# A state-space scan beside a local attention on one core: frames of four tokens with scaled B and C, and masks on GpSimd

## The chip, the cores and the metric

The kernel runs on one core of one Trainium2 chip. The metric is the device time in microseconds (us) of one execution. The kernel before takes 249.55 us as the median of four runs. Each run is marked fast or slow: a run is slow when it lies more than 1.5% above the fastest of its kernel.

Names of the engines in the profile: PE does the matrix products (PEld is its weight load), DVE is the vector engine, ACT the scalar engine, POOL is GpSimd, and SP is the engine from which most transfers are issued.

## The reference, cut to what matters

The two halves of the output are independent. The inputs and the output are bf16; S is 2048 and the width is 448.

```python
# Part A: a diagonal complex state-space layer, 448 complex states
dt = exp(log_dt); Lam_bar = exp(dt * Lam)
B_bar = ((Lam_bar - 1) / Lam)[:, None] * Bmat
Bu = x @ B_bar.T                                   # complex
for t in range(2048):
    h = Lam_bar * h + Bu[t]                        # the scan
y = 2 * (hseq @ Cmat.T).real + x * Dskip

# Part B: attention, 16 heads of 28; token t sees t, t-2, ..., t-14
q, k, v = split(x @ wqkv)
logits = q . k at 8 positions with stride 2, times 28 ** -0.5; positions < 0 masked
o = softmax(logits) @ v;   out = o @ wo

output = concatenate([A, B], axis=-1)
```

In both kernels the complex state is kept as 128 partitions (64 real, 64 imaginary) times 7 groups m.

Of the kernel before, what the change touches and what calls it, by code (L numbers as in the profile page):

```python
# [11 lines left out]
AX = mybir.AxisListType  # L12
# [3 lines left out]
S = 2048  # L16
D = 448
T = 16
NCH = 128
KT = 4  # L20
KP = 112
H = 16
DH = 28
W = 8
DIL = 2
HALO = (W - 1) * DIL
JH = T * H
TJ = HALO + T
NM = 7
PL = 64  # L30
NST = 7
PAD = 64
MA = 4
# [3 lines left out]
COSC = [(-1.0) ** k / math.factorial(2 * k) for k in range(7, 0, -1)]  # L37


def _make_identity(nc, ident):  # L40
    n = ident.shape[0]
    nc.gpsimd.memset(ident, 0.0)
    nc.gpsimd.affine_select(
        out=ident, in_=ident, compare_op=ALU.not_equal, fill=1.0, base=0,
        pattern=[[-1, n]], channel_multiplier=1,
    )


class PartB:

    QB = 114
    HL = 14
    XP = 16
    XC = XP + S + 16
    NB = 18
    GROUPS = ((0, 4), (4, 4), (8, 4), (12, 4), (16, 2))

    def __init__(self, tc, B_x, B_wqkv, B_wo, out_b, ident, pool, psum):
        self.tc, self.nc = tc, tc.nc
        self.B_x, self.B_wqkv, self.B_wo, self.out_b = B_x, B_wqkv, B_wo, out_b  # L60
        self.ident, self.pool, self.psum = ident, pool, psum

    def loads(self):
        nc, pool = self.nc, self.pool
        self.xT = pool.tile([NCH, KT, self.XC], bf16, name="xbT_sb", tag="xbT")
        for c in range(2):
            rows = slice(1024 * c, 1024 * (c + 1))
            cols = slice(self.XP + 1024 * c, self.XP + 1024 * (c + 1))
            nc.sync.dma_start_transpose(self.xT[:, 0:3, cols], self.B_x[0, rows, 0:384])  # L69
            nc.sync.dma_start_transpose(self.xT[:, 3, cols], self.B_x[0, rows, 320:448])  # L70
        self.wn = pool.tile([NCH, KT, 3 * D], bf16, name="wqkv_nat", tag="wn")
        nc.gpsimd.memset(self.wn[0:64, 3, :], 0.0)
        nc.scalar.dma_start(self.wn[:, 0:3, :], self.B_wqkv[0:384].rearrange("(k p) c -> p k c", p=NCH))
        nc.scalar.dma_start(self.wn[64:128, 3, :], self.B_wqkv[384:448])

    def loads2(self):
        nc, pool = self.nc, self.pool
        self.wo_p = pool.tile([NCH, 4, D], bf16, name="wo_p")
        nc.gpsimd.memset(self.wo_p[:], 0.0)
        wo_v = self.B_wo.rearrange("(g h d) c -> h d g c", g=4, d=DH)  # L80
        for h in range(4):
            nc.scalar.dma_start(self.wo_p[32 * h:32 * h + DH, :, :], wo_v[h])

    def prep(self):
        nc, pool, V, G = self.nc, self.pool, self.nc.vector, self.nc.gpsimd
        G.memset(self.xT[:, :, 0:self.XP], 0.0)
        G.memset(self.xT[:, :, self.XP + S:], 0.0)
        self.wp = pool.tile([NCH, 2, KT, H, 32], bf16, name="wqk_p", tag="xin")
        G.memset(self.wp[:, :, :, :, DH:], 0.0)
        for w in range(2):  # L90
            V.tensor_copy(self.wp[:, w, :, :, 0:DH],
                          self.wn[:, :, w * D:(w + 1) * D].rearrange("p k (h d) -> p k h d", d=DH))
        self.qT = pool.tile([NCH, 4, S], bf16, name="qT")
        self.kT = pool.tile([NCH, 4, self.XC], bf16, name="kT")
        G.memset(self.kT[:, :, 0:self.XP], 0.0)
        G.memset(self.kT[:, :, self.XP + S:], 0.0)
        self.va = pool.tile([NCH, self.NB, H, 32], bf16, name="v_aug")
        G.memset(self.va[:, :, :, DH:], 0.0)
        self.ones = pool.tile([NCH, 2, 32], bf16, name="ones")
        G.memset(self.ones[:], 1.0)  # L100
        G.memset(self.ones[0:self.HL, 1, :], 0.0)
        self.mask = pool.tile([NCH, self.QB], bf16, name="mask")
        G.memset(self.mask[:], 0.0)
        for w in range(W):
            G.affine_select(out=self.mask[:], in_=self.mask[:], compare_op=ALU.not_equal, fill=1.0,
                            base=self.HL - DIL * w, pattern=[[1, self.QB]], channel_multiplier=-1)
        self.oT = pool.tile([NCH, 4, self.XC], bf16, name="oT", tag="xbT")

    def qk_proj(self, c):
        nc = self.nc  # L110
        n = 0
        for w in range(2):
            for hg in range(4):
                ps = self.psum.tile([NCH, 512], f32, name="qk_ps", tag="mm")
                for k in range(KT):
                    nc.tensor.matmul(ps[:], lhsT=self.wp[:, w, k, 4 * hg:4 * hg + 4].rearrange("p h d -> p (h d)"),  # L116
                                     rhs=self.xT[:, k, self.XP + 512 * c:self.XP + 512 * (c + 1)],
                                     start=(k == 0), stop=(k == KT - 1))
                if w == 0:
                    dst = self.qT[:, hg, 512 * c:512 * (c + 1)]  # L120
                else:
                    dst = self.kT[:, hg, self.XP + 512 * c:self.XP + 512 * (c + 1)]
                if n % 2 == 0:
                    nc.scalar.copy(dst, ps[:])  # L124
                else:
                    nc.vector.tensor_copy(dst, ps[:])  # L126
                n += 1

    def v_proj(self, g):
        nc = self.nc  # L130
        b0, nb = self.GROUPS[g]
        for b in range(b0, b0 + nb):
            c0 = self.QB * b + self.XP - self.HL
            ps = self.psum.tile([NCH, H, DH], f32, name="v_ps", tag="mm")
            for k in range(KT):
                nc.tensor.matmul(ps[:].rearrange("p h d -> p (h d)"), lhsT=self.xT[:, k, c0:c0 + NCH],  # L136
                                 rhs=self.wn[:, k, 2 * D:3 * D], start=(k == 0), stop=(k == KT - 1))
            if b % 2 == 0:
                nc.scalar.copy(self.va[:, b, :, 0:DH], ps[:])
            else:  # L140
                nc.vector.tensor_copy(self.va[:, b, :, 0:DH], ps[:])

    def unit(self, g, hg):
        nc, pool, V = self.nc, self.pool, self.nc.vector
        b0, nb = self.GROUPS[g]
        QB, XP, HL = self.QB, self.XP, self.HL
        scale = DH ** -0.5
        nq = [min(QB, S - QB * b) for b in range(b0, b0 + nb)]
        tot = sum(nq)
        sp = [self.psum.tile([NCH, 2, 512], f32, name="s_ps", tag="s") for _ in range(2)]  # L150
        for i in range(nb):
            b = b0 + i
            kc = QB * b + XP - HL
            for h in range(4):
                nc.tensor.matmul(sp[h // 2][:, h % 2, QB * i:QB * i + nq[i]],  # L155
                                 lhsT=self.kT[32 * h:32 * h + DH, hg, kc:kc + NCH],
                                 rhs=self.qT[32 * h:32 * h + DH, hg, QB * b:QB * b + nq[i]],
                                 start=True, stop=True, skip_group_check=True)
        pts = []
        for u in range(2):  # L160
            pt = pool.tile([NCH, 2, 4 * QB], bf16, name="pt", tag="pt", bufs=4)
            nc.scalar.activation(pt[:, :, 0:tot], sp[u][:, :, 0:tot], ACT.Exp, scale=scale)  # L162
            if tot == nb * QB:
                pv = pt[:, :, 0:tot].rearrange("p h (b q) -> p h b q", q=QB)
                V.tensor_tensor(pv, pv, self.mask[:].unsqueeze(1).unsqueeze(1).to_broadcast([NCH, 2, nb, QB]),  # L165
                                op=ALU.mult)
            else:
                pv = pt[:, :, 0:QB]
                V.tensor_tensor(pv, pv, self.mask[:].unsqueeze(1).to_broadcast([NCH, 2, QB]), op=ALU.mult)
                pv = pt[:, :, QB:tot]  # L170
                V.tensor_tensor(pv, pv, self.mask[:, 0:nq[1]].unsqueeze(1).to_broadcast([NCH, 2, nq[1]]), op=ALU.mult)
            pts.append(pt)
        po = self.psum.tile([NCH, 4 * QB], f32, name="o_ps", tag="mm")
        pd = self.psum.tile([NCH, 4 * QB], f32, name="d_ps", tag="mm")
        for i in range(nb):
            for h in range(4):
                nc.tensor.matmul(po[32 * h:32 * h + 32, QB * i:QB * i + nq[i]],  # L177
                                 lhsT=self.va[:, b0 + i, 4 * hg + h, :],
                                 rhs=pts[h // 2][:, h % 2, QB * i:QB * i + nq[i]],
                                 start=True, stop=True, skip_group_check=True)  # L180
        spl = ((0, QB, 1), (QB, tot, 0)) if b0 == 0 else ((0, tot, 0),)
        for lo, hi, o in spl:
            for h in range(4):
                nc.tensor.matmul(pd[32 * h:32 * h + 32, lo:hi], lhsT=self.ones[:, o, :],  # L184
# [30 lines left out]
    def attention(self):  # L215
        done = 0
        for g, (b0, nb) in enumerate(self.GROUPS):
            for hg in range(4):
                self.unit(g, hg)
# [385 lines left out]
```

## The kernel before: the parts that the change touches

Part A walks through 16 steps j. All 128 chunks of 16 tokens advance one step at a time; the state is carried by products with a high and a low part of a rotation matrix; each state goes to memory and is read back, corrected with the result of the scan over the chunks, and used for y.

```python
def _level1_step(self, j, prev, has_prev):              # 16 times
    for m in range(NM):
        for k in range(KT):                             # 28 products of 128 columns
            nc.tensor.matmul(reg(m), lhsT=self.Bcat[:, k, m, :], rhs=self.xT[:, k, j, :], ...)
    if has_prev:
        for m in range(NM):                             # 14 carry products
            nc.tensor.matmul(reg(m), lhsT=Lm[:, m, :], rhs=prev(m), ...)
            nc.tensor.matmul(reg(m), lhsT=Lm[:, NM + m, :], rhs=prev(m), ...)
    nc.scalar.copy(ht[:, 0:MA, :], psA[:])
    nc.scalar.copy(ht[:, MA:NM, :], psB[:])
...
# main(): states to memory and back, correction, y
for j in range(T):
    eng.dma_start(hin[:].rearrange("p m c -> p (m c)"), hs[j])
    for m in range(NM):
        nc.tensor.matmul(reg(m), lhsT=ident[:], rhs=hin[:, m, :], ...)
        nc.tensor.matmul(reg(m), lhsT=cm, rhs=g, ...)
    nc.scalar.copy(ht[:, 0:MA, :], psA[:]); nc.scalar.copy(ht[:, MA:NM, :], psB[:])
    ... # y from 7 products with Ccat and 4 with the skip, ACT copies it out
```

Part B works in 20 units: a group of up to four blocks of queries times one of four groups of heads. The mask is a DVE multiply, the denominators are products with ones, and the reciprocal is Ln and Exp on ACT.

```python
nc.scalar.activation(pt[...], sp[u][...], ACT.Exp, scale=scale)
V.tensor_tensor(pv, pv, self.mask[...].to_broadcast(...), op=ALU.mult)
...                                                     # o_ps: weights times v
for h in range(4):
    nc.tensor.matmul(pd[32 * h:32 * h + 32, lo:hi], lhsT=self.ones[:, o, :], rhs=pts[h // 2][...], ...)
nc.scalar.activation(r[:, 0:tot], pd[:, 0:tot], ACT.Ln)
nc.scalar.activation(r[:, 0:tot], r[:, 0:tot], ACT.Exp, scale=-1.0)
V.tensor_tensor(self.oT[...], po[:, 0:tot], r[:, 0:tot], op=ALU.mult)
```

The order in which the parts are written is: projections of B, weights of A, all of A, all of B's attention.

The softmax here doesn't subtract the row's maximum and nothing guards it: scores larger than these inputs give would overflow.

## Time and profile before

| | before |
|---|---|
| median time | 249.55 us (248.87 to 250.39, 4 runs) |
| span of the profiled run | 247.0 us |
| PE, DVE, ACT, POOL busy | 199.7, 67.9, 139.0, 36.3 us |
| written to memory | 7.34 MB |

From the page of the kernel before: busy time of each engine (with its share of the span and its instructions), and the chain of waits that ended last, by engine.

```profile
PE 199.7 (81%) x2261; PEld 127.5 (52%) x2261; DVE 67.9 (27%) x157; ACT 139.0 (56%) x261; POOL 36.3 (15%) x54
...
PE 47%; ACT 24%; issue 11%; DVE 8%; SPq 7%; DMA 2%; ACTq 0%
```

The windows view of the kernel before gives, for each stretch from:to, its length, the busy us of each engine (x is the count of instructions), the granted clock of PE as a share of full speed, the DMA share and GB/s.

```profile
0.00:37.00 37.00, 16.48 (x64) 6.05 (x65) 16.44 (x66) 7.84 (x15) 13.59 (x41) 0.92 0.85 166
37.00:71.00 34.00, 33.65 (x156) 15.51 (x156) 18.04 (x25) 13.83 (x21) 22.75 (x13) 0.93 0.10 36
71.00:85.00 14.00, 12.39 (x168) 10.19 (x166) 0.62 (x1) 13.79 (x29) 0.00 (x0) 1.00 0.12 49
85.00:120.00 35.00, 35.00 (x630) 35.00 (x627) 1.27 (x2) 17.05 (x35) 0.00 (x0) 1.00 0.34 113
120.00:136.00 16.00, 11.37 (x181) 9.74 (x177) 0.00 (x0) 11.58 (x25) 0.00 (x0) 1.00 0.09 31
136.00:181.00 45.00, 38.75 (x386) 25.95 (x386) 0.00 (x0) 21.86 (x47) 0.00 (x0) 1.00 0.37 106
181.00:247.00 66.00, 52.04 (x692) 25.07 (x688) 31.51 (x64) 53.04 (x93) 0.00 (x0) 0.79 0.09 31
```

The order of the five busy columns is PE, PEld, DVE, ACT, POOL. PE is busy 33.65 of 34 us in B's projections and 35.00 of 35 in level 1 of A; ACT is busy 13.79 of 14 in the set-up between them; in the attention at the end PE and ACT share the load. DVE and POOL stand idle for whole stages.

These are lines of the timeline of before on DVE and on POOL around 38 us (start, duration, engine, line, operation):

```profile
37.89 3.23 DVE L165 TENSOR_TENSOR pt<-pt,mask 128x912 bf16<-128x912 bf16 x1
...
37.45 3.19 POOL L384 TENSOR_TENSOR Lmat<-Dm,Shl 128x1792 bf16<-128x1792 f32 x1 [1.14 <-DVE gs L398]
```

The mask multiply takes 0.744 us on the mean of its 32 executions, but 3.23 us when it meets a POOL instruction of 3.19 us: it ended only after the POOL instruction had.

### The profile page before, as it was taken

The page shows a single profiled execution, that of the slowest core. Times are in us where ns is not written, and L with a number is a line of the kernel's source. Part 1 is how long each engine was busy: PE and PEld are TensorE (multiplying, and loading weights), DVE is VectorE, ACT ScalarE, POOL GpSimd, SP SyncE. Part 2 cuts the span into 40 slices and gives each one's busy share as a digit, 9 for nine tenths or more (in the row PEclk, how much of TensorE's full clock was granted, in tenths as well). Part 3 has the DMA queues.
Part 4 walks back from the last instruction along what each step waited for, and adds up shares of the span by engine and source line. Part 5 has one row for each costly group of instructions (what it writes and reads, how often), then busy time and mean ns, then how long its engine had stood idle before and what let it go on. Part 6 is the DMA issues. An engine that isn't in the chain of part 4 may idle for free.

```text
span 247.0 us, 5315 instructions
## 1 busy us (share of the span) xinstructions
PE 199.7 (81%) x2261; PEld 127.5 (52%) x2261; DVE 67.9 (27%) x157; ACT 139.0 (56%) x261; POOL 36.3 (15%) x54
## 2 busy tenths in 40 slices
PE   0282939999999899999777888888859798697983
PEld 0030313444468699999766555556534443344341
DVE  0204999543330020000000000000024464655450
ACT  2002435523369964344568554444577898989782
POOL 9400089997000000000000000000000000000000
PEclk9999786999999999999999999999995958977687
DMA  7977940000170036323200344444110101102021
GB/s 210 174 151 133 221 102 1 3 0 0 23 277 1 3 89 211 107 84 114 89 28 0 93 118 128 123 118 136 38 40 0 39 0 42 35 3 77 1 76 37
DMA packets 24592, 19.30 MB, mean 78 GB/s; under 512 B 12664, under 2 KB 23992, under 8 KB 24440
## 3 DMA queue, kind: packets, MB, share of 16 engines
q1 hardware_dynamic: 23584, 17.36, 26.5%
q10 hardware_dynamic: 984, 1.61, 2.3%
q8 instruction: 17, 0.28, 0.5%
q14 instruction: 7, 0.06, 0.1%
HBM read 9.53 MB, written 7.34 MB: 68 GB/s over the span
## 4 chain that ended last, share of the span: by engine, by line
PE 47%; ACT 24%; issue 11%; DVE 8%; SPq 7%; DMA 2%; ACTq 0%
PE qk_ps L116 9%; PE wo_ps L195 6%; PE l1A L433 6%; SPq L69 5%; PE v_ps L136 4%; PE l1B L433 4%; ACT pt L162 4%; PE y_ps L518 4%; ACT ya L524 3%; ACT xaT_sb L457 3%; PE o_ps L177 3%; ACT yb L199 2%; PE s_ps L155 2%; PE d_ps L184 2%; DVE pt L165 2%
## 5 line engine op out<-in xcount | busy, mean ns | idle before, releaser
L165 DVE TENSOR_TENSOR pt<-pt,mask 128x912 bf16<-128x912 bf16 x32 | 23.8, 744 | 130.1 <-ACT pt L162 129.2
L116 PE MATMUL qk_ps<-xbT_sb,wqk_p 128*128 128x512 bf16 x128 | 35.2, 437 | 17.0 <-DMA xbT_sb<-in_B_x_dram 11.6
L162 ACT ACTIVATE pt<-s_ps 128x912 bf16<-128x912 f32 (+1 forms) x40 | 34.6, 883 | 4.0 <-PE s_ps L155 3.9
L116 PEld LDWEIGHTS <-wqk_p 128*128 128x128 bf16 x128 | 14.0, 109 | 37.7 <-issue 18.2
L433 PEld LDWEIGHTS <-Bcat 112*128 112x128 bf16 x448 | 25.7, 98 | 0.2 <-issue 0.2
L524 ACT CAST ya<-y_ps 128x448 bf16<-128x448 f32 x16 | 8.5, 532 | 23.4 <-issue 20.6
L155 PE MATMUL s_ps<-qT,kT 28*128 28x114 bf16 (+1 forms) x288 | 16.5, 231 | 5.2 <-ACT pt L162 4.8
L195 PE MATMUL wo_ps<-wo_p,oT 128*128 128x448 bf16 x64 | 19.8, 449 | 0.9 <-DVE oT L189 0.9
L443 ACT CAST ht<-l1A 128x512 bf16<-128x512 f32 x16 | 9.7, 603 | 19.3 <-issue 18.0
L136 PE MATMUL v_ps<-wqkv_nat,xbT_sb 128*128 128x448 bf16 x72 | 15.5, 365 | 3.8 <-DVE kT L126 3.8
L155 PEld LDWEIGHTS <-kT 28*128 28x128 bf16 x288 | 9.3, 99 | 16.6 <-issue 14.6
L124 ACT CAST qT<-qk_ps 128x512 bf16<-128x512 f32 x8 | 4.7, 583 | 22.2 <-PE qk_ps L116 22.2
L433 PE MATMUL l1A<-xaT_sb,Bcat 112*128 112x128 bf16 x256 | 16.9, 219 | 0.1
L384 POOL TENSOR_TENSOR Mmat<-Dm,Scat 128x896 bf16<-128x896 f32 x7 | 12.4, 1798 | 21.7 <-DVE Scat L376 21.7
L184 PE MATMUL d_ps<-pt,ones 128*32 128x456 bf16 (+3 forms) x96 | 14.6, 378 | 0.9 <-ACT r L187 0.8
L177 PE MATMUL o_ps<-pt,v_aug 128*32 128x114 bf16 (+1 forms) x288 | 12.5, 246 | 3.2 <-DVE pt L165 2.7
L187 ACT ACTIVATE r<-d_ps 128x456 f32<-128x456 f32 (+1 forms) x20 | 10.5, 528 | 5.3 <-PE d_ps L184 5.1
L433 PE MATMUL l1B<-xaT_sb,Bcat 112*128 112x128 bf16 x192 | 13.3, 219 | 0.0
L177 PEld LDWEIGHTS <-v_aug 128*32 128x32 bf16 x288 | 7.9, 105 | 9.3 <-issue 6.4
L136 PEld LDWEIGHTS <-xbT_sb 128*128 128x128 bf16 x72 | 7.0, 99 | 10.8 <-issue 4.5
L189 DVE TENSOR_TENSOR oT<-o_ps,r 128x456 bf16<-128x456 f32 (+1 forms) x20 | 11.5, 579 | 3.9 <-ACT r L188 3.9
L195 PEld LDWEIGHTS <-oT 128*128 128x128 bf16 x64 | 6.1, 113 | 10.3 <-issue 6.5
(211 smaller groups left out, 359.3 us busy)
## 6 DMA issues: line engine op xcount, KB each, us to landing
hs<-ht SPq DMA_DIRECT2D x16, 224.0 KB, 2.1
hin<-hs SPq DMA_DIRECT2D x16, 224.0 KB, 2.6
xa_sb<-in_A_x_dram SPq DMA_DIRECT2D x1, 1792.0 KB, 8.0
out_dram<-ya SPq DMA_DIRECT2D x16, 112.0 KB, 1.7
out_dram<-yb SPq DMA_DIRECT2D x8, 224.0 KB, 2.1
wqkv_nat<-in_B_wqkv_dram ACTq DMA_DIRECT2D x1, 1008.0 KB
wo_p<-in_B_wo_dram ACTq DMA_DIRECT2D x4, 98.0 KB
bX<-in_A_B_re_dram SPq DMA_DIRECT2D x1, 392.0 KB, 4.7
```

The costliest lines, as they stand in the source:

```text
L69: nc.sync.dma_start_transpose(self.xT[:, 0:3, cols], self.B_x[0, rows, 0:384])
L116: nc.tensor.matmul(ps[:], lhsT=self.wp[:, w, k, 4 * hg:4 * hg + 4].rearrange("p h d -> p (h d)"), rhs=self.xT[:, k, self.XP + 512 * c:self ...
L136: nc.tensor.matmul(ps[:].rearrange("p h d -> p (h d)"), lhsT=self.xT[:, k, c0:c0 + NCH], rhs=self.wn[:, k, 2 * D:3 * D], start=(k == 0), s ...
L155: nc.tensor.matmul(sp[h // 2][:, h % 2, QB * i:QB * i + nq[i]], lhsT=self.kT[32 * h:32 * h + DH, hg, kc:kc + NCH], rhs=self.qT[32 * h:32 * ...
L162: nc.scalar.activation(pt[:, :, 0:tot], sp[u][:, :, 0:tot], ACT.Exp, scale=scale)
L165: V.tensor_tensor(pv, pv, self.mask[:].unsqueeze(1).unsqueeze(1).to_broadcast([NCH, 2, nb, QB]), op=ALU.mult)
L177: nc.tensor.matmul(po[32 * h:32 * h + 32, QB * i:QB * i + nq[i]], lhsT=self.va[:, b0 + i, 4 * hg + h, :], rhs=pts[h // 2][:, h % 2, QB * i ...
L184: nc.tensor.matmul(pd[32 * h:32 * h + 32, lo:hi], lhsT=self.ones[:, o, :], rhs=pts[h // 2][:, h % 2, lo:hi], start=True, stop=True, skip_g ...
L195: nc.tensor.matmul(ps[:], lhsT=self.oT[:, hg, NCH * t:NCH * (t + 1)], rhs=self.wo_p[:, hg, :], start=(hg == 0), stop=(hg == 3))
L384: eng.tensor_tensor(out_tile, Dm[:].unsqueeze(1).unsqueeze(1).to_broadcast([NCH, n, 2, PL]), scal.unsqueeze(3).to_broadcast([NCH, n, 2, PL ...
L433: nc.tensor.matmul(reg(m), lhsT=self.Bcat[:, k, m, :], rhs=self.xT[:, k, j, :], start=(k == 0 and m in (0, MA)), stop=(not has_prev and k ...
L524: nc.scalar.copy(ya[:], yps[:])
```

## The change

The intent is to take work off PE and ACT and to run A beside B. Part A is redone in frames of 4 tokens: the discretised B is scaled by the inverse powers 0 to -3 of the rotation, so that the sum over the 4 steps of a frame builds up in PSUM with no carry; C is scaled by the powers 0 to 3; what is left is one small scan over the frames, and the states never leave the core. Part B goes by parity of the token (a stride of 2 becomes a band of 8), the mask is two affine selects on POOL, the denominator is 4 columns of ones in v, and the normalisation is two DVE transposes with a reciprocal and a multiply between them. The new order interleaves units of B with the parts of A. The core of the diff, with cuts marked:

```diff
 # Part B, unit
-            V.tensor_tensor(pv, pv, self.mask[...], op=ALU.mult)
+            G.affine_select(out=pv, in_=pv, compare_op=ALU.is_ge, fill=0.0, base=-1,
+                            pattern=[[0, 2], [0, nb], [-1, nq]], channel_multiplier=1)
+            G.affine_select(out=pv, in_=pv, compare_op=ALU.is_ge, fill=0.0, base=HALO,
+                            pattern=[[0, 2], [0, nb], [1, nq]], channel_multiplier=-1)
-        for lo, hi, o in spl: ...  nc.tensor.matmul(pd[...], lhsT=self.ones[:, o, :], ...)
-        nc.scalar.activation(r[:, 0:tot], pd[:, 0:tot], ACT.Ln)
-        nc.scalar.activation(r[:, 0:tot], r[:, 0:tot], ACT.Exp, scale=-1.0)
-        V.tensor_tensor(self.oT[...], po[:, 0:tot], r[:, 0:tot], op=ALU.mult)
+        V.transpose(tO[:, 0:nj].rearrange("p j d -> p (j d)"), po[:, 0:tot])
+        V.reciprocal(r[:, 0:nj], tO[:, 0:nj, DH])
+        V.tensor_tensor(on[:, 0:nj], tO[:, 0:nj], r[...].to_broadcast([P, nj, 32]), op=ALU.mult)
+        V.transpose(oT[:, hg, 0:tot], on[:, 0:nj].rearrange("p j d -> p (j d)"))
 # Part A, weights (C likewise, three sets of 7)
+    def b_variant(self, s):                             # 4 sets of 7
+        for m in range(NM):
+            ...                                         # st = bX * sa, on ACT or DVE
+            eng.scalar_tensor_tensor(st[:, m, :], self.bY[:, m, :], self.sb[:, s, m:m + 1], st[:, m, :],
+                                     op0=ALU.mult, op1=ALU.add)
+        nc.sync.dma_start_transpose(self.Bv[s][:], st[:].rearrange("p m c -> p (m c)"))
 # Part A, level 1
-    def _level1_step(self, j, prev, has_prev): ...      # 16 steps with carries
+    def l1(self, j):
+        for s in range(4):
+            for u, m in enumerate(ms):
+                for k in range(KT):                     # products of 512 columns, PSUM sums over s
+                    nc.tensor.matmul(ps[u][:], lhsT=self.Bv[s][:, KT * m + k, :], rhs=self.xT[:, k, s, :],
+                                     start=(s == 0 and k == 0), ...)
 # ... scan (l2), frame offsets (hfull), y: cut
 # order
-    b.projections(); a.setup_c(); a.setup_weights(); b.loads2(); a.main(); b.attention()
+    b.proj(0); a.b_variant(0); a.loads_c(); # four units of group 0
+    b.proj(1); a.b_variant(1); a.loads_x(); a.b_variant(2); b.loads2(); a.b_variant(3); a.mats(G)
+    # four units of group 1; b.proj(2); b.wo(0)
+    for hg in range(4): b.unit(2, hg); a.l1(hg)
+    # b.proj(3); b.wo(1); a.l2(); four units of group 3; b.wo(2)
+    a.c_variants()
+    for m in range(NM): a.hfull(m)
+    b.proj(4)
+    for s in range(4):
+        b.unit(4, s)
+        for i in range(4): a.y(i, s)
```

## The prediction

> **What bounds it now.** The windows view splits 247.0 us into stages that follow one another: start 0-37 (PE busy 16.5), B's projections 37-71 (PE 33.7 of 34), C and x set-up 71-85 (ACT 13.8 of 14), level 1 85-120 (PE 35.0 of 35), scan 120-136 (PE and ACT wait for each other), correction and y 136-181 (PE 38.8 of 45), attention 181-247 (PE 52, ACT 53 of 66, granted clock 0.79). The chain of waits is 47% PE, 24% ACT, 11% issue. DVE (67.9 us) and POOL (36.3, nothing after 60) are nearly idle. So PE bounds most stages; A and B hardly overlap.
>
> **Removed, by chain throughput** (56 ns per 128-column matmul, about 190 per 448-column one): 210 carry matmuls of level 1, 11.8 us; correction, 224, 12.5; identity adds of the scan and Ga, 4; x, B and C transposes and products, 8.6; denominators, 8. On ACT: Ln and Exp 21.7 us, x copies 8, state copies of level 1 and correction about 35. Also the DRAM round trip of the states (2 x 3.7 MB). Added on PE: about 7 us (end sums, frame offsets, 18 output blocks for 16). I estimate PE's true work at 165 -> 130 us.
>
> **Added.** DVE: 28 + 21 scale-and-add of 512/448 columns (0.63 and 0.57 us, estimated from the 456-column multiply, 0.627), 30 us; normalise per unit about 2 us (two transposes, reciprocal, multiply), 36; scan adds and frame adds, 20; evictions 20, set-up 15: about 125 us. ACT: about 110. POOL: 80 affine selects. The trace has them only at 114-128 columns, 288-346 ns, memsets at 0.88 ns per column; I estimate 1.25 us for 960 columns (1.0-1.6), 0.6 for 384: 90 us; with matrices (10 x 1.7), memsets, and DMA issue about 130 us.
>
> **Critical path.** PE is no longer the limit; POOL and DVE are, and they exclude each other. The Trainium skill, "SBUF — State Buffer", has the shared port pair as an exclusive lock held for a whole instruction, against DVE instructions with two SBUF inputs. The trace agrees: the mask multiply took 3.23 us beside a 3.19 us POOL multiply (0.744 mean, all 32), and a 7-column copy 1.68 us. So POOL's SBUF-reading work (about 110 us) and DVE's two-input work (about 55) add up to some 165 us, not overlapped; with 12 us at the start, 8 at the tail and 20-25 of gaps (in-order waits, one output PSUM buffer, three others) I get about 204. The kernel gains from overlap and less PE work, but loses part of it to that lock.
>
> **Prediction: 204 us, 178 to 232.** Faster by over 2%: 0.91; within 2%: 0.04; slower: 0.05.
>
> **What would show it.** POOL busy above 50% of the span, from some 20 us to near the end; full selects 1.0-1.6 us; two-input DVE operations (normalise multiply, scale-and-add) well above their 0.6 us while PSUM-source operations keep theirs; DVE 140-170 us busy; PE's share of the chain below 35%, POOL and DVE above 40% together; HBM bytes written about 3.7 MB instead of 7.34; PE busy about 150-165.
>
> **What would make it wrong.** Selects at 2 us or more: POOL alone 180 us, time 230-250. Selects below 1 us, or no lock against them: 175-180. SP's in-order queue: 20 DMA transposes more (issue 1.3-7.3 us each in the trace), those of C waiting for thousands of 128-byte pieces, could hold up level 1's weights and x, and put A's serial tail (level 1, scan, frames, y) last.

## The result, and the profile after

The kernel after is correct and takes 232.82 us (median of 4 runs, 231.25 to 234.02) beside 249.55 us of the kernel before. The ratio is 0.9325, with a 95% interval of 0.9246 to 0.9403. Ratios here and below are the mean time of one kernel's fast runs over that of the other's of the same rounds, so they are not quite the ratio of the quoted medians. The gain is 16.7 us where 45.5 us were predicted, and the time lies just above the predicted range, which ended at 232.

Page of the kernel after: busy times and the chain of waits, by engine and then by line.

```profile
PE 162.8 (71%) x1298; PEld 83.2 (36%) x1298; DVE 152.8 (66%) x271; ACT 102.9 (45%) x179; POOL 129.1 (56%) x149
...
DVE 35%; PE 26%; POOL 11%; ACT 9%; issue 2%; DMA 1%; ACTq 0%; DVEq 0%
DVE st L381 15%; PE y_ps L468 7%; POOL pt L162 6%; PE l_ps L409 6%; DVE on L180 5%; POOL pt L164 3%; DVE st L380 3%; PE o_ps L170 3%; DVE Dv_1839 L393 3%; ACT pt L160 3%; PE wo_ps L189 3%; PE qk_ps L120 2%; DVE tO L176 2%; DVE oT L181 2%; POOL cP L397 2%
```

Every busy time lies at or near where the prediction put it: PE 162.8 (150 to 165), DVE 152.8 (140 to 170), POOL 129.1 or 56% (about 130, over 50%), ACT 102.9 (about 110). Memory writes fell to 3.67 MB. PE has 26% of the chain, POOL and DVE together 46%. The sums are right and the time is not. The windows view of the kernel after shows the reason in outline:

```profile
0.00:33.00 33.00, 12.98 (x64) 5.59 (x65) 15.80 (x75) 8.82 (x17) 17.54 (x48) 0.84 1.11 182
33.00:98.00 65.00, 40.01 (x332) 16.87 (x331) 64.69 (x71) 32.18 (x51) 58.85 (x43) 0.76 0.65 118
98.00:135.00 37.00, 34.81 (x274) 15.17 (x273) 18.77 (x33) 19.03 (x31) 17.18 (x20) 1.00 0.05 13
135.00:148.00 13.00, 12.36 (x86) 7.54 (x85) 10.93 (x19) 13.00 (x27) 0.00 (x0) 1.00 0.09 24
148.00:184.00 36.00, 22.53 (x213) 12.62 (x211) 30.97 (x51) 15.33 (x25) 27.63 (x23) 0.59 0.06 16
184.00:226.00 42.00, 39.63 (x338) 25.31 (x337) 11.66 (x26) 13.45 (x30) 7.91 (x16) 0.95 0.16 52
```

DVE and POOL are full together in the second stretch (groups 0 and 1 of the units, B's weights and the matrices) and nearly so in the fifth (group 3, C's weights). In level 1 (98 to 135) and in the y stage (184 to 226) PE is busy 34.8 of 37 and 39.6 of 42 us, and POOL and DVE have little to do; in between ACT is busy 13.00 of 13. So the kernel after is still a sequence of stages, each with a limit of its own.

Groups of the kernel after in which DVE and POOL wait for each other (the lock of the prediction; L381 is the scale-and-add of B's weights, L162 is a select, L365 makes the matrices of the scan, L180 is the normalise multiply; line, engine, operation, output and inputs, shape, count | busy us, mean ns | idle before):

```profile
L162 POOL TENSOR_SCALAR_AFFINE_SELECT pt<-pt 128x960 bf16<-128x960 bf16 x16 | 19.1, 1215 | 21.7 <-ACT pt L160 21.7
L381 DVE SCALAR_TENSOR_TENSOR st<-bY,sb,st 128x512 bf16<-128x512 bf16 x28 | 38.4, 1408 | 0.0
L365 POOL TENSOR_TENSOR Mm<-Dm,Sc 128x896 bf16<-128x896 bf16 x10 | 19.5, 1980 | 12.9 <-DVE Sc L355 12.9
L180 DVE TENSOR_TENSOR on<-tO,r 128x480 bf16<-128x480 f32 x8 | 9.7, 1216 | 0.1
```

The timeline of the kernel after, on DVE and on POOL around 36 us, shows how the two take turns:

```profile
34.54 0.73 DVE L381 SCALAR_TENSOR_TENSOR st<-bY,sb,st 128x512 bf16<-128x512 bf16 x1
35.73 9.64 DVE L381 SCALAR_TENSOR_TENSOR st<-bY,sb,st 128x512 bf16<-128x512 bf16 x7
...
37.58 2.93 POOL L164 TENSOR_SCALAR_AFFINE_SELECT pt<-pt 128x960 bf16<-128x960 bf16 x2
40.46 2.93 POOL L162 TENSOR_SCALAR_AFFINE_SELECT pt<-pt 128x960 bf16<-128x960 bf16 x2
```

One scale-and-add takes 0.73 us while POOL has no select. Seven in a row take 9.64 us, 1.38 each, while POOL's selects take 2.93 us a pair where two alone take about 2.0 (1.04 us each in experiment e5). So each waits for the other, as the prediction said. The Trainium skill, "SBUF — State Buffer", section "Who interferes with whom", describes this lock; the trace agrees. Not the whole of both durations is exclusive, though: a turn of 1.46 us is shorter than the 0.73 + 1.04 = 1.77 us of the two alone. And more than the two-input work was caught: the scaling of B with one SBUF tensor as input (L380) took 0.35 us at 33 us, before the selects, and 0.96 to 1.77 us beside selects and matrices.

### The profile page after: what moved, and what is told of

Same layout as the page of the kernel before. It is cut to its first block, busy times and chain, and to the rows that moved or that the text cites. A ratio compares the mean times of both kernels' runs of the same rounds, so it can differ in the third digit from the quotient of the medians.

```text
span 229.9 us, 3506 instructions
## 1 busy us (share of the span) xinstructions
PE 162.8 (71%) x1298; PEld 83.2 (36%) x1298; DVE 152.8 (66%) x271; ACT 102.9 (45%) x179; POOL 129.1 (56%) x149
## 3 DMA queue, kind: packets, MB, share of 16 engines
HBM read 3.22 MB, written 3.67 MB: 30 GB/s over the span
## 4 chain that ended last, share of the span: by engine, by line
DVE 35%; PE 26%; POOL 11%; ACT 9%; issue 2%; DMA 1%; ACTq 0%; DVEq 0%
DVE st L381 15%; PE y_ps L468 7%; POOL pt L162 6%; PE l_ps L409 6%; DVE on L180 5%; POOL pt L164 3%; DVE st L380 3%; PE o_ps L170 3%; DVE Dv_1839 L393 3%; ACT pt L160 3%; PE wo_ps L189 3%; PE qk_ps L120 2%; DVE tO L176 2%; DVE oT L181 2%; POOL cP L397 2%
## 5 line engine op out<-in xcount | busy, mean ns | idle before, releaser
L162 POOL TENSOR_SCALAR_AFFINE_SELECT pt<-pt 128x960 bf16<-128x960 bf16 (+2 forms) x40 | 41.6, 1062 | 59.2 <-ACT pt L160 59.2
L160 ACT ACTIVATE pt<-s_ps 128x960 bf16<-128x960 f32 (+2 forms) x40 | 32.1, 859 | 40.0 <-PE o_ps L170 21.4
L164 POOL TENSOR_SCALAR_AFFINE_SELECT pt<-pt 128x960 bf16<-128x960 bf16 (+2 forms) x40 | 41.4, 1058 | 0.0
L381 DVE SCALAR_TENSOR_TENSOR st<-bY,sb,st 128x512 bf16<-128x512 bf16 x28 | 38.4, 1408 | 0.0
L120 PE MATMUL qk_ps<-xb_66,wqk_p 128*128 128x480 bf16 (+5 forms) x96 | 23.5, 392 | 19.1 <-ACT qT L125 9.6
L170 PE MATMUL o_ps<-pt,va 128*32 128x120 bf16 (+2 forms) x288 | 12.7, 251 | 29.1 <-DVE tO L176 16.5
L365 POOL TENSOR_TENSOR Mm<-Dm,Sc 128x896 bf16<-128x896 bf16 x10 | 19.5, 1980 | 12.9 <-DVE Sc L355 12.9
L170 PEld LDWEIGHTS <-va 128*32 128x32 bf16 x288 | 8.0, 108 | 42.7 <-issue 22.1
L120 PE MATMUL qk_ps<-xb_67,wqk_p 128*128 128x480 bf16 (+5 forms) x96 | 21.6, 363 | 1.9 <-ACT qT L125 1.9
L176 DVE STREAM_TRANSPOSE tO<-o_ps 128x480 f32<-128x480 f32 (+2 forms) x20 | 12.0, 600 | 12.8 <-PE o_ps L170 12.7
L189 PE MATMUL wo_ps<-wo_p,oT 128*120 128x448 bf16 (+2 forms) x72 | 18.5, 404 | 0.0
L180 DVE TENSOR_TENSOR on<-tO,r 128x480 bf16<-128x480 f32 (+2 forms) x20 | 18.3, 917 | 0.3
L153 PE MATMUL s_ps<-qT,kT 28*128 28x120 bf16 (+2 forms) x288 | 14.6, 234 | 0.6 <-ACT pt L160 0.5
```

The lines of the kernel that those rows point to most:

```text
L120: nc.tensor.matmul(ps[:, off:off + cnt], lhsT=self.wp[:, w, k, 4 * hg:4 * hg + 4].rearrange("p h d -> p (h d)"), rhs=self.xb[p][:, k, XP + ...
L153: nc.tensor.matmul(sp[h // 2][:, h % 2, nq * i:nq * (i + 1)], lhsT=kT[32 * h:32 * h + DH, hg, koff[i]:koff[i] + P], rhs=qT[32 * h:32 * h + ...
L160: nc.scalar.activation(pt[:, :, 0:tot], sp[u][:, :, 0:tot], ACT.Exp, scale=scale)
L162: G.affine_select(out=pv, in_=pv, compare_op=ALU.is_ge, fill=0.0, base=-1, pattern=[[0, 2], [0, nb], [-1, nq]], channel_multiplier=1)
L164: G.affine_select(out=pv, in_=pv, compare_op=ALU.is_ge, fill=0.0, base=HALO, pattern=[[0, 2], [0, nb], [1, nq]], channel_multiplier=-1)
L170: nc.tensor.matmul(po[32 * h:32 * h + 32, nq * i:nq * (i + 1)], lhsT=va[:, i, 4 * hg + h, :], rhs=pts[h // 2][:, h % 2, nq * i:nq * (i + 1 ...
```

## The experiments

Three theories, all of them named in the expectations below, can account for the missing 28.8 us.

- **Lock theory:** the lock costs more than was thought. Then taking the lock away while all the work stays must give the time back.
- **Stage theory:** the kernel is a row of stages with different limits, and in the two stages where DVE and POOL are busy there is more than one full chain. Then taking one chain's load away gives nothing unless the others have room, and the PE stages stay as long as they are.
- **POOL-latency theory:** in every unit the product with v waits for the exponentials and then for the selects, one after the other; their own length holds up the units, whether DVE waits or not. Then taking selects out helps, and taking DVE's waits away does not.

A useful mark is the start of the first level 1 product (level 1 is A's product of x with B's weights): 100.2 us in the kernel after. What follows it took 229.9 - 100.2 = 129.7 us of the span.

### e1: one select instead of two

```diff
-            G.affine_select(out=pv, in_=pv, ..., base=HALO, ..., channel_multiplier=-1)
```

> The second of the two GpSimd selects of every half unit is left out (wrong result on purpose, 40 selects and about 41 us of POOL less). Lock theory (POOL and DVE take turns on the shared port): the scale-and-add of the B weights, 1.41 us mean in the changed kernel, falls to about 1.1, DVE busy falls from 153 to about 135, time falls by 8 to 15 us to 218-225. POOL-latency theory (the selects hold up the units, DVE's waits do not matter): DVE's durations hardly move, time falls by 10 us or more through shorter units. Stage theory (PE stages of level 1 and y come after the DVE stages and are untouched): the gap between 98 and 135 us and the y stage keep their lengths, about 37 and 42 us.

Measured: 214.02 us, ratio 0.8575 (0.8507 to 0.8643). The result is wrong by design, since the far side of the band is not masked. POOL was busy 87.0 us instead of 129.1, the scale-and-add took 1.179 us instead of 1.408, level 1 began at 88.5 us. Half the selects are worth 18.8 us: the selects are on the path. DVE's durations fell as the lock theory has it, but the time lies below its 218 to 225; the run does not tell that theory from the POOL-latency theory.

### e2: the mask as a DVE multiply again

```diff
-            G.affine_select(...); G.affine_select(...)
+            V.tensor_tensor(pv, pv, self.mask[:, 0:nq]..., op=ALU.mult)
```

> The masks go back to one DVE multiply per half unit (right result; POOL 83 us less, DVE 40 multiplies of about 0.68 us, 26 us more). Lock theory: the waits of DVE's two-input work (about 20 us in the B scale-and-adds, 8 in the normalise multiplies, 5 in the C scale-and-adds) go away and about pay for the 26 us: time 225-235, the same as the changed kernel within 2 to 3%, DVE busy 140-155. POOL-latency theory: taking four selects of 1.2 us in series out of every unit shortens the units: 215 or less.

Measured: 214.75 us, ratio 0.8622 (0.8562 to 0.8683); correct. POOL fell to 44.3 us busy. DVE took 22.1 us of mask multiplies on and was busy 157.3 us, hardly more than the 152.8 before them, because its waits went: the scale-and-add took 0.744 us. Level 1 began at 87.5 us. So all the masks on the fuller of the two engines beat the same masks on POOL. The time is that of the POOL-latency theory (215 or less) and not that of the lock theory (225 to 235). But the work is not the same: the multiplies took 22.1 us where the selects had taken 83.0, so cheaper masks and missing waits are not separated here.

### e3: the mask as a product on PE

The exponent gets -2000 outside the band, by one product with the identity per head, before the scores are summed into the same PSUM.

```diff
+        for h in range(4):
+            nc.tensor.matmul(sp[h // 2][:, h % 2, 0:tot], lhsT=self.ident[:], rhs=self.bias[nq][...],
+                             start=True, stop=False)
         ...                                             # the scores: start=False
-            G.affine_select(...); G.affine_select(...)
```

> The masks become a bias of -2000 added on PE before the exponential (right result; POOL 83 us less, DVE nothing more, PE 4 products of 192-480 columns per unit, about 15 us more). Lock theory: B scale-and-add mean falls from 1.41 to 0.7-0.9 us (the matrices of POOL are still there), normalise multiply from 0.92 to about 0.6, DVE busy from 153 to about 120, the end of the B weights from 91 us to about 75; time 205-215. If the lock did not matter and only POOL latency did: DVE durations unchanged. Stage theory: of the 83 us of POOL work taken away less than 25 us is seen in the time, since level 1 and y stay PE-bound.

Measured: 212.19 us, ratio 0.8508 (0.8442 to 0.8573); correct. DVE 138.0 us busy, POOL 47.6; the scale-and-add took 0.733 us and the normalise multiply 0.574 on the mean of its three shapes, 0.917 in the kernel after. Level 1 began at 92.8 us, later than in e1 and e2, and the profile shows why. Timeline of e3, DVE and POOL:

```profile
29.08 16.25 DVE L343 TENSOR_TENSOR tb<-ch,sb 128x21 f32<-128x21 f32 x1
45.25 0.17 DVE L345 TENSOR_TENSOR sb<-kf,sb 128x21 f32<-128x21 f32 x1
...
30.49 14.80 POOL L374 TENSOR_TENSOR Mm<-Dm,Sc 128x896 bf16<-128x896 bf16 x9
```

A DVE multiply of 21 columns, which takes 0.17 us, stood for 16.25 us, until nine POOL multiplies that followed each other without a gap were done. In e2 the same ten multiplies let DVE in after each one. Here the lock was not passed in turn. The wait began 1.4 us before the nine multiplies, while POOL was issuing four transfers, and so it did, by 1.2 us, in the like cases of e7 and e8; in e2 no transfers stood among the multiplies. Whether they have a part in it was not tested. What followed the start of level 1 took 210.7 - 92.8 = 117.9 us of the span instead of 129.7, so the stages after it gained as well.

### e4: group 3 of the units between the y products

```diff
-    # units of group 3, then c_variants, hfull, proj(4), then per s: unit(4, s), y(0..3, s)
+    # c_variants, hfull; per s: unit(3, s), y(0, s), y(1, s), y(2, s), y(3, s), with proj(4) and units of group 4 among them
```

> Only the order of the program changes (right result, the same instructions): the units of group 3 are traced after the frame sums, between the y products, so that their POOL and DVE work may run beside the PE-bound y stage instead of ahead of it. Stage theory: the DVE and POOL stage from 148 to 183 us shortens by 10 to 20 us and time falls to 212-222, with the same busy time of POOL and DVE within 5%. If the sum of locked work is what bounds the whole kernel: time stays at 228-233.

Measured: 229.37 us, ratio 0.9191 (0.9119 to 0.9262). This is a miss, and the time is that of the other reading, the sum of the locked work (228 to 233). But the edit did only part of what it was meant to: in the timeline of e4, 12 of the 16 selects of group 3 still ran from 157.7 to 172.7 us, ahead of y, and only those of one unit, from 210.3 us on, among the y products. So the run decides nothing about the order. Level 1 began at 99.8 us as before.

### e5: the lock taken away, the work kept

ACT writes its half of the scaled B to PSUM instead of SBUF, so that the scale-and-add reads only one operand from SBUF.

```diff
-            # st = bX * sa on ACT or DVE, in SBUF
+            tp = self.psum.tile([P, 512], f32, name="bv_ps", tag="mm")
+            nc.scalar.activation(tp[:], self.bX[:, m, :], ACT.Copy, scale=self.sa[:, s, m:m + 1])
             eng.scalar_tensor_tensor(st[:, m, :], self.bY[:, m, :], self.sb[:, s, m:m + 1],
-                                     st[:, m, :], ...)
+                                     tp[:], ...)
```

> The cleanest test of the lock: all GpSimd work stays, and the 28 scale-and-adds of the B weights stay, but ACT writes the scaled half into PSUM, so that each has one SBUF input and one PSUM input instead of two SBUF inputs (right result; 12 more ACT copies, 12 fewer DVE scalings). Lock theory: the scale-and-add falls from 1.41 us mean to 0.60-0.72 while the selects beside it run, selects fall from 1.21 to about 1.05-1.1, the last B weights are ready at 75-83 us instead of 91, time 216-224. If DVE was slowed by POOL in another way (shared bandwidth, clock): the scale-and-add stays above 1.1 and time stays at 228-233.

Measured: 231.37 us, ratio 0.9286 (0.9217 to 0.9354); correct. The wait is gone. Group of the scale-and-add in e5, and the page's chain by engine and by line:

```profile
L379 DVE SCALAR_TENSOR_TENSOR st<-bY,sb,bv_ps 128x512 bf16<-128x512 bf16 x28 | 19.1, 734 | 3.1 <-ACT bv_ps L378 3.1
```

```profile
PE 28%; POOL 25%; DVE 18%; ACT 15%; DMA 7%; issue 3%; SPq 2%; ACTq 0%; DVEq 0%
POOL pt L162 10%; POOL pt L164 8%; PE y_ps L466 7%; PE l_ps L407 6%; PE qk_ps L120 5%; POOL Mm L365 4%; ACT bv_ps L378 4%; ACT pt L160 4%; DMA dsk_raw<-in_A_Dskip_dram 3%; PE o_ps L170 3%; DVE Dv L391 3%; DMA lre_raw<-in_A_Lambda_re_dram 3%; ACT Dv L390 3%; DVE hl L460 2%; DVE on L180 2%
```

The scale-and-add takes 0.734 us instead of 1.408, DVE's busy time fell by 23.8 us (152.8 to 129.0), POOL's by 10.5, and level 1 began at 99.9 us against 100.2. DVE's share of the chain fell from 35% to 18%, and POOL's rose from 11% to 25%. The lock is real, and its waits can be taken away; the start of level 1 did not follow. But the test is not as clean as its text says. It also takes 12 scalings off DVE, and its PSUM tiles come out of the same three buffers as those of B's projections. PE's longest wait in e5 between 33 and 98 us (engine, line, what it waited for: us in total, times, longest), and POOL's first selects in e5 and, below, in the kernel after:

```profile
PE qk_ps L120 <- DVE st L379: 14.5, 2, 11.1
42.32 1.04 POOL L162 TENSOR_SCALAR_AFFINE_SELECT pt<-pt 128x960 bf16<-128x960 bf16 x1 [6.86 <-ACT pt L160]
35.00 2.62 POOL L162 TENSOR_SCALAR_AFFINE_SELECT pt<-pt 128x960 bf16<-128x960 bf16 x2 [3.94 <-ACT pt L160]
```

PE stood idle 14.5 us for buffers that the scale-and-adds held, which it did not do in the kernel after, and the first select began 7 us later. What the lock's waits alone are worth is therefore not measured by e5; e6 has to be read beside it.

### e6: B's weights made on PE

```diff
-        # scale and scale-and-add, then a transpose by DMA
+        # g: diagonal matrices of sa and sb, made by two DVE multiplies per set
+        nc.tensor.matmul(ps[:, k, :], lhsT=src_[:, m, P * k:P * (k + 1)], rhs=g[:, h, m, :], ...)   # bX, bY
+        # ACT or DVE copies ps to Bv
```

> The four B weight sets are made on PE from diagonal matrices as in the kernel before (right result; 224 products of 128 columns, about 12.5 us of PE; DVE loses 28 scale-and-adds and 12 scalings, 47 us with their waits, and gets 8 wide multiplies and 12 evictions, about 16; four transposing DMAs go). Theory that the DVE chain of the B weights gates level 1: DVE busy 115-125, the stage before level 1 ends at about 82 us instead of 98 (then bound by POOL's selects of eight units and its matrices, about 50 us from 31), time 212-220. If level 1 was held by the POOL selects ahead of it in PE's order instead: time 225 or more.

Measured: 230.77 us, ratio 0.9279 (0.9222 to 0.9335); correct. It takes away DVE's 28 scale-and-adds and four transposes of the SP queue, and adds 224 products on PE. Level 1 began at 99.0 us. POOL had 28% of the chain. From 33 to 100 us POOL's selects and matrices were 57% of it. The first select began at 35.95 us, so e5's late start is not there, and DVE's chain and its DMA transposes are gone; level 1 still began no earlier. The time lies in the second reading (225 or more), that the selects ahead of level 1 in PE's order hold it up. The edit also adds PE work before level 1.

### e7 and e8: mask and weights on PE, without and with a new order

e7 is e3 and e6 together. e8 is e7 with level 1 beside the units of group 1 instead of group 2 and the y products among groups 3 and 4.

```diff
     for hg in range(4):
         b.unit(1, hg)
+        a.l1(hg)
+    # b.proj(2), b.wo(0), a.l2(), a.c_variants(), units of group 2, b.proj(3), hfull
     for s in range(4):
+        b.unit(3, s); a.y(0, s); a.y(1, s); a.y(2, s); a.y(3, s)   # units of group 4 among them
```

> e3 and e6 together (right result): neither the selects nor the scale-and-adds are there. DVE busy 100-112, POOL below 50, PE busy about 170-180. If both causes hold up the first 98 us, level 1 starts at 65-72 us and the time is 190-200. If, once the selects are gone, something else sets the start of level 1 (loads, ACT, PE order), the time is 203-212, no better than e3.

> e7 with the program's order changed so that each PE-heavy part stands beside units (level 1 beside group 1, scan and frames beside group 2, y beside group 3 and 4; right result). Stage theory: PE's idle stretches (the scan and the C weights, about 25 us with PE below 80% in e3) shrink, time 178-190. If PE's own work is the bound by now: PE busy above 85% of the span. If order does not matter, within 2% of e7.

Measured: e7 222.81 us, ratio 0.8957 (0.8904 to 0.9009); e8 213.36 us, ratio 0.8577 (0.8524 to 0.8631); both correct. Neither run met a reading of its text: e7 lies above both ranges, and e8 above 178 to 190 with PE busy 81% of the span. The new order was worth 9.5 us. e7 is slower than e3, although DVE has less to do. In both, a DVE multiply of 7 columns stood 16.03 and 16.04 us behind the POOL multiplies for the matrices. What that costs is estimated by e15 and e16 below, which differ from e7 and e8 only in where the matrices are made.

### e9 and e10: the matrices on DVE

```diff
-    a.mats(G)
+    a.mats(V)
```

e9 is the kernel after with this edit, e10 is e5 with it.

> Only the ten block matrices of the scan move from GpSimd to DVE (right result; POOL loses 19.5 us between 29 and 74 us, DVE gets ten multiplies, 8-12 us). Theory now: level 1 starts (100 us in the changed kernel) when PE has passed the units of groups 0 and 1, which needs both POOL's queue up to there (32 selects and the matrices, 58 us from 33) and DVE's chain (B weights, normalising, with waits, 58 us); the later of the two sets it. POOL's part falls to 32 selects at 1.0-1.3 us, DVE's stays about the same (8-12 us more work, fewer waits): level 1 starts at 92-99, time 222-230. If POOL's queue alone set it: level 1 at 80-86, time 211-217.

> e5 and e9 together (right result): the scale-and-adds take one operand from PSUM, so they wait for no select, and POOL has no matrices before level 1. Alone, e5 gave nothing. If two parallel queues set the start of level 1, both are now shorter: level 1 starts at 82-90 us and the time is 212-220. If something else (loads, the projection on PE) sets it: level 1 stays at 98-100, time 228-232.

Measured: e9 230.45 us, ratio 0.9233 (0.9174 to 0.9292). e10 229.08 us, ratio 0.9185 (0.9140 to 0.9231). e10 takes the waits off DVE and the matrices off POOL and still gains only about 3 us on the kernel after; its level 1 began at 98.4 us. That is the second reading, that something other than two parallel queues sets the start. Between 33 and 98 us POOL was busy only 36.7 us and DVE 48.3 of 65, while PE waited 15.3 us for selects and 12.4 us for exponentials: this fits the POOL-latency theory. (The first select began late here too, at 40.36 us, behind a POOL memset that waited for the transfer of C.) The selects, which e10 keeps, are worth 18 us or more by e1 to e3.

### e11 and e12: e3 with the matrices on DVE, without and with the new order

```diff
-    a.mats(G)
+    a.mats(V)                                           # e11 on e3; e12 has the order of e8 too
```

> e3 with the matrices on DVE (right result). In e3 one 21-column DVE multiply stood 16.25 us while nine POOL matrix multiplies ran back to back, so the B weights began at 47 us instead of 34. Without them that wait must go: level 1 starts at 79-85 us instead of 92.8, time 197-205. If the wait was not what delayed e3: time 210-214.

> e11 with the order of e8 (right result): level 1 beside group 1, scan, C weights and frames beside group 2, y beside group 3. Order was worth 9.5 us in e8 against e7, so 188-196. PE busy above 80% of the span.

Measured: e11 219.52 us, ratio 0.8819 (0.8764 to 0.8875); e12 213.54 us, ratio 0.8563 (0.8521 to 0.8605). The stop of 16 us is gone in e11, and yet it is 7 us slower than e3, which was not foreseen. In e11 the chain has 15% DMA and 14% SP's queue: the first transpose of B's weights was issued at 55.67 us, behind transposes of x and C, and ACT's next scaling, which waits for the buffer, holds the exponentials behind it (ACT waited 14.28 us for that transpose); PE stood idle for 12.67 us at one place. e12 missed its range, 188 to 196, as well, with PE busy 78% of the span; the order was worth 6.0 us. So SP's queue became a suspect, which the next runs test.

### e13, e14: the SP order, by the order of the text

```diff
-    b.load_x(1, 0); b.load_x(1, 1)                      # before b.prep()
-    a.loads_c()                                         # after b_variant(0)
     a.b_variant(3)
+    b.load_x(1, 0); b.load_x(1, 1); a.loads_c()
```

e13 is the kernel after with this edit, e14 is e11 with it.

> Only the order of SP's queue is changed in the kernel after (second half of B's x and C's loads and transposes are issued after B's weight transposes). If the selects on POOL hold level 1, its first matmul stays at 99 to 101 us and the time at 229 to 233 us. If SP's queue is what holds it already in the kernel after, level 1 starts at 90 us or before and the time is 220 to 224.

> e11 (mask on PE, matrices on DVE) with SP's new order. If the DMA issue queue was what made e11 late, the transposes of B's second and third set land some 10 to 15 us sooner, level 1 starts at 80 to 88 us instead of 97.5, and the time is 203 to 211 instead of 219.5. If DVE's chain or PE is what holds level 1, it stays at 94 to 98 and the time at 216 to 220.

Measured: of e13 only one run was fast, the profiled one, 230.76 us, with level 1 at 99.8; the other three, 234.83 to 237.47, are slow, so no interval is quoted. e14: 220.86 us, ratio 0.8862 (0.8822 to 0.8901), level 1 at 99.7. The runs are inconclusive for their question, because the edit did not do what it was meant to: the framework's scheduler arranges the queue itself. SP's own timeline in e14 shows that B's first transpose was still issued after those of x and C:

```profile
48.26 1.26 SPq L75 DMA_TRANSPOSE xb<-in_B_x_dram  x1
49.62 5.23 SPq L261 DMA_TRANSPOSE cP<-cn  x4
54.94 4.20 SPq L393 DMA_TRANSPOSE Bv<-st  x1
```

### e15 and e16: everything taken off POOL, DVE's chain and SP at once

e15 is e7 with the matrices on DVE; e16 is e8 with the matrices on DVE. In both the masks and B's weights are made on PE.

```diff
-    a.mats(G)
+    a.mats(V)                                           # e15 on e7, e16 on e8
```

> Mask on PE, B weights made on PE, matrices on DVE, order of work as in the kernel after. No queue but PE's has much to do before level 1. If the queues held it, level 1 starts at 80 to 88 us and the time is 198 to 208. If PE is now full before level 1 (18 us of weight products and 5 of mask products more than the kernel after), it starts at 92 or later and the time is 211 or more.

> e15 with level 1 beside the units of the second group. e8, which differs by the matrices on POOL and their 16 us stop of DVE, took 213.4. If that stop cost what it lasted, this one takes 196 to 203; if PE is the limit all the way (its busy time in e8 was 19.7 of 20 us from 60 us on), the stop was partly hidden and it takes 205 to 212.

Measured: e15 210.06 us, ratio 0.8416 (0.8373 to 0.8460); e16 200.97 us, ratio 0.8045 (0.7989 to 0.8100); both correct. Windows of e15 and, below, of e16:

```profile
45.00:91.00 46.00, 45.72 (x527) 26.76 (x528) 33.12 (x53) 30.20 (x50) 1.24 (x4) 1.00 0.41 74
91.00:125.00 34.00, 33.43 (x247) 14.63 (x250) 17.90 (x30) 18.30 (x29) 0.31 (x1) 1.00 0.01 4
```

```profile
60.00:80.00 20.00, 19.56 (x224) 11.89 (x224) 11.32 (x18) 10.74 (x17) 0.00 (x0) 1.00 0.07 15
140.00:160.00 20.00, 19.84 (x193) 11.82 (x191) 11.47 (x18) 11.08 (x21) 0.00 (x0) 1.00 0.17 52
```

In e15 PE is busy 45.72 of the 46 us before level 1, which begins at 90.9 us: both this start and the time of 210.06 lie between the figures of the two readings, but PE is full, which only the second reading has. e16 lies within the range of its first reading, that the stop of DVE had cost about what it lasted. Two results follow. Making the matrices on DVE, which takes the stop away, was worth 222.81 - 210.06 = 12.8 us in one pair and 213.36 - 200.97 = 12.4 us in the other. If the stop is what changed it, it cost most of the 16 us that it lasted; that no other effect of the move plays in is not shown (from e3 to e11 the same move lost 7 us). And e16, which takes 19.5% less time than the kernel before by its ratio, is the best version; it beats both kernels.

### e17 and e18: the SP order, forced

Edges in the program now hold the transposes of x and C behind those of B. The Trainium skill, "DMA: Bandwidth & Descriptors", section "DMA Transpose (X-bar)", says that a plain DMA transpose can be issued from SP or ACT only, so moving it to an idle POOL was not tried, and no run here shows what would happen. e17 is e11 with the forced order, e18 the kernel after with it.

```diff
+    with tc.issue_after(<B's transpose s>):
+        ...  # s = 0: A's x, two steps; 1: the rest of it; 2: B's second x; 3: C
```

> e11 (mask on PE, matrices on DVE) with SP's queue forced: B transpose 0, A's x for two steps, B transpose 1, the rest of A's x, B transpose 2, B's second x, B transpose 3, then C. If the SP queue held e11 and e14, the first B transpose is issued at 44 to 48 us instead of 55, the hole of PE at 48 to 61 us closes, level 1 starts at 84 to 92 us and the time is 203 to 212. If DVE's chain or PE holds it, the time stays at 216 to 221.

> The kernel after with the same forced order of SP's queue, nothing else changed. If selects, matrices and DVE's waits hold the stage before level 1, as the e1 to e3 results say, level 1 stays at 97 to 102 us and the time at 228 to 233. If SP's queue was part of the limit in the kernel after, level 1 starts at 92 or before and the time is 218 to 225.

Measured: e17 219.75 us, ratio 0.8796 (0.8724 to 0.8868). Its profiled run was slow (222.86), so only the order of its queue is read from it:

```profile
44.66 4.30 SPq L394 DMA_TRANSPOSE Bv<-st  x1
49.00 1.47 SPq L248 DMA_TRANSPOSE xa<-in_A_x_dram  x1
...
86.89 5.24 SPq L262 DMA_TRANSPOSE cP<-cn  x4
```

B's first transpose now leaves at 44.66 us, 11 us earlier than in e11, and the time did not follow. e18: 242.22 us; two of its four runs were fast, 239.35 and 240.34, and the two slow ones were 244.11 and 244.69, so no ratio is given. (One of seven runs of the kernel before beside them took 776 us; it is left out.) In the fast, profiled run of e18 level 1 began at 108.1 us. B's second x, now behind B's transposes, was issued from 83.24 us on, where the kernel after had issued it by 32 us; the projections that need it stand on the chain from 91.4 us. e17 lies at its second reading, that the order is not the limit; e18 was foreseen by neither of its readings. No order of the SP queue that was tried is the missing gain, and a wrong order costs.

## Why the prediction was right or wrong, point by point

**Right: the lock and its size.** Two-input DVE operations were to be well above 0.6 us beside the selects: the scale-and-add took 1.408 us, and 0.734 without a second SBUF operand (e5), the normalise multiply 1.216 at 480 columns. Full selects were put at 1.0 to 1.6 us: 1.215 with waits, 1.04 in e5.

**Right: the sums.** Busy times, bytes and shares of the chain came out as forecast; they are listed with the result. "Selects at 2 us or more" did not happen.

**Wrong: the step from the sums to the time.** The prediction said "PE is no longer the limit; POOL and DVE are", added 165 us of locked work "not overlapped" to 12 us of start, 8 of tail and 20 to 25 of gaps, and so came to 204. It expected POOL to be busy "from some 20 us to near the end". The windows of the kernel after give the real terms:

| term | predicted us | in the profile us |
|---|---|---|
| start, until DVE and POOL are both full | 12 | 33 (0 to 33) |
| stages in which DVE and POOL are the limit | 165 | 101 (65 + 36) |
| gaps (prediction); stages between those two, limited by PE or ACT (profile) | 20 to 25 | 50 (37 + 13) |
| after the last of them | 8 | 46 (184 to 229.9) |
| sum | 205 to 210, given as about 204 | 230 |

The pairing of the prediction's terms with the stages is ours. The locked term was too large: of POOL's selects, matrices and signs of C (113 us busy, waits included, foreseen as about 110), 25.7 us ran outside those two stages (1.7 in the start, 16.1 in level 1, 7.9 in the y stage). The other three were too small by about 87 us together. In level 1 and in the y stage PE was the limit: it was busy 74.4 of 79 us there, more than a third of the span. One sum for the whole span supposes that work of one stage may fill the gaps of another; here level 1 needs all of B's weights, and y needs C's weights and the scan, and in this order most of it did not. Another order was worth 9.5, 6.0 and 9.1 us (e8, e12, e16), though only in kernels that have the masks on PE. The prediction had split the kernel before into stages, and did not do the same for the kernel after.

**Part of the same step, and in part argued: what holds the stage before level 1.** DVE's chain of weights and POOL's chain of selects and matrices ran side by side there, busy 64.7 and 58.9 of 65 us with their waits for each other. The chain of waits of the kernel after, from 33 to 98 us, and that of e5 over the same stretch, by line (the view cuts the second off at its edge):

```profile
by line: DVE st L381 54.7%; DVE on L180 10.5%; DVE st L380 10.3%; DVE tO L176 4.4%; PE v_ps L131 4.0%; DVE oT L181 3.6%; DVE va L137 3.2%; PE wo_ps L189 2.9%; issue 2.8%; PE o_ps L170 2.2%; DVE r L178 0.9%
```

```profile
by line: POOL pt L164 17.1%; POOL Mm L365 15.8%; POOL pt L162 15.2%; ACT bv_ps L378 14.7%; PE qk_ps L120 10.8%; ACT pt L160 4.9%; PE v_ps L131 4.7%; DMA out_dram<-yb 2.9%; PE o_ps L170 2.5%; DVE tb L334 2.5%; DVE sb L329 2.5%; DVE on L180 1
```

When DVE no longer waited, POOL's lines made up 48% of the chain over the same 65 us, ACT's scaling 15% and B's projections 11%. e5, e6, e9 and e10, which keep the selects, gained only 1 to 4 us; e1 to e3, which take selects away and with them a part (e1) or most (e2, e3) of DVE's waits, gained 18 to 21. So the selects on POOL are what the time follows. That POOL's queue was a second chain as long as DVE's is not shown: POOL was busy 46.7 of the 65 us in e5 and 36.7 in e10, and level 1 did not begin sooner than 98.4 us. The selects in series inside each unit (POOL-latency theory) fit these runs better; no run takes the selects out and leaves DVE's waits, so the two are not separated. When POOL, DVE's chain of B's weights and SP were all relieved (e15), PE was full.

**Foreseen in size, without a reason: PE's busy time.** The prediction put PE's true work at 130 us and its busy time at 150 to 165. The kernel after shows 162.8 us busy. Taking from e16's 171.7 us the products it adds (20.7 for the masks, 29.8 for B's weights) leaves 121.2. The rest, about 42 us, is the same products taking longer where PE waits between them, as far as the profile tells (it models their ends). One group of the output product that shows it, in the kernel after and in e16 (the other large group of that line, 128*112, does not: 353 and 362 ns):

```profile
L189 PE MATMUL wo_ps<-wo_p,oT 128*120 128x448 bf16 x32 | 10.6, 469 | 0.0
```

```profile
L198 PE MATMUL wo_ps<-wo_p,oT 128*120 128x448 bf16 x32 | 6.7, 353 | 0.0
```

The Trainium skill, "TensorE: Matmul & The Clock Gate", Part 1, says that PE's clock is held at half until the engine has been busy for some microseconds. The windows agree in direction: the granted clock was 0.76 where PE was busy 40 of 65 us, 0.59 at 22.5 of 36, and 1.00 in level 1. How much of the 42 us lay on the path was not measured alone.

**The named risks.** "SP's in-order queue" was not found to hold up level 1 in the kernel after: with B's transposes first (e18) it was slower, though e18 also held up B's second x. "A's serial tail last" did come true, in the y stage of 42 us; the order of the stages is the likelier cause, since e8, e12 and e16 gained by it and no order of the queue did.

**What stays open.** How much of the stage before level 1 is the selects' own length and how much DVE's waits, as said above. With the masks on PE and the matrices on DVE (e11, e14, e17), the time stays at 219.5 to 220.9 us whichever way the SP queue is ordered, while e15 without B's chain and its transposes takes about 10 us less. Whether DVE's and ACT's part of that chain or the transposes matter more was not separated, since e15 takes both away.

## What to carry to other kernels

Split the kernel after into its stages too, and ask of each which queues run side by side in it: taking one engine's waits away gave 1 to 4 us here while the selects stayed, and an average busy share cannot show that. Two engines that exclude each other make a poor pair for sharing one stage's work; moving all the mask work to the fuller engine (e2) or to a third (e3) was worth 18 to 21 us here, in part because the mask itself became cheaper (22.1 us for 83.0 in e2). Do not let a long row of back-to-back POOL instructions stand beside small DVE work that everything waits for.

## What the Trainium skill lacked or had wrong

- "SBUF — State Buffer": whoever starts first is said to hold the pair for its whole instruction. It lacks who is next. In e3 a waiting two-input DVE multiply of 21 columns was passed over by nine successive POOL multiplies, 16.25 us (16.03 and 16.04 in e7 and e8); moving the multiplies away gained 12.8 and 12.4 us there. In the kernel after, scale-and-adds and selects took turns about one for one (1.38 us for each of the one, 1.46 for each of the other).
- "GPSIMD Engine Reference": it gives no duration for an affine select. The runs show about 1.04 us for 128x960 bf16 with little lock waiting (L162 in e5) and 1.215 with it (the kernel after); 0.530 for 128x384.
- "DMA: Bandwidth & Descriptors": it gives a transpose's decode and execution time in the sequencer in cycles, for other sizes, but no time in us for one like this. Here the SBUF-to-SBUF transpose of one set of B's weights (128x3584 bf16) held SP's queue for 4.1 to 5.0 us (the kernel after, e11, e14, e17, e18) and landed 6.1 to 7.8 us after issue in the kernel after.
- "TensorE: Matmul & The Clock Gate": nothing wrong was found; the granted clock of 0.59 to 0.76 in stages where PE waits fits it.
